# A delta-rule attention woven into a feed-forward: spreading VectorE's work of a step's first burst over the stretch behind it

## The chip, the cores and the metric

The kernel runs on one core of one Trainium2 chip. The metric is the device time in microseconds (us) of one execution. TensorE is called PE in the profile (its weight loads PEld), VectorE DVE, ScalarE ACT, GpSimd POOL and SyncE SP. `L867` is line 867 of the kernel before the change.

## The reference

Two blocks follow one another. The first is a delta rule over 768 positions, for 4 batches x 8 heads of width 48; the second is a feed-forward over the 3072 tokens of width 384 that the first one gives, with 2048 hidden units and a slope of its own for each unit below zero.

```python
k_n = k / (np.linalg.norm(k, axis=-1, keepdims=True) + 1e-06)
for t in range(S):
    y[:, :, t] = einsum('bhd,bhde->bhe', q[:, :, t], state)
    v_old = einsum('bhde,bhd->bhe', state, kt)
    state = state + bt * einsum('bhd,bhe->bhde', kt, vt - v_old)
x = attn_out.transpose(0, 2, 1, 3).reshape(B * S, H * D)
h = x @ w_in
g = np.maximum(h, 0.0) + alpha * np.minimum(h, 0.0)
return g @ w_out
```

All of it is in float32.

## The kernel before

**Steps.** The 768 positions are cut into 12 chunks of 64. A step is one chunk of one pair of batches, so there are 24 steps; even steps are the first pair of batches, odd steps the second. Within a chunk the recurrence is turned into matrix products and an inverse of a triangular matrix. A step n needs: keys times state (`through_state`, L793), whose result gives the right-hand side r (three subtractions, L812) and the masked matrix a_t (L521); `solve` (L824), whose result DVE weighs into u (L831); `outputs` (L836), copied to y (ACT at L848 up to step 15, DVE at L847 from step 16 on); and `next_state` (L853), subtracted from the state by DVE (L867, two instructions, one in the first steps). The state of a pair of batches is next read two steps later.

**Way of a step's result.** From step 8 on y is turned in 32x32 blocks by one DVE instruction (`turn_y`, L883, into z), and 16 small ACT copies (`rows_y`, L896) put the rows of z into xt, the feed-forward's input of a chunk. The odd step completes a chunk. z shares a tag of two buffers with r.

**The feed-forward** is a generator, `tail`, cut into parts; each part issues some matmuls of PE, and now and then DVE and ACT instructions. For chunks 2 to 7 (`ffn_in`, L989, and `ffn_out_fast`, L1051) a pair of hidden tiles takes 6 parts, one PSUM bank, one ACT relu (L1008) and two DVE instructions (L1010). From chunk 8 on (`ffn_in_fast`, L1201, `ffn_out_faster`, L1306) products are combined as in Strassen's scheme, and a pair i takes 6 parts: the common products (L1247) go into one PSUM bank that all pairs share, ACT copies the bank to a tile z_i (L1266; two tiles, called k_t and block in the profile, take turns), POOL adds three times in it (L1271), DVE adds it to the pair's own products (`total`, L1276), ACT takes the part below zero (L1281) and DVE puts in the slopes (L1285, two instructions). `Due` counts parts and says behind which part a total, a below and a slope is issued: the total of pair i stands some 3 parts behind the pair.

**Order of the work.** The order on every engine is written out by hand; the queues run in order. From step JOINED = 6 on, the loop at L1926 does for each step:

- `burst_a(n)`: PE gets outputs(n-1), next_state(n-1) and through_state(n) in a row, and then DVE gets all that reads them, in a row: the list `soon`, run by `now(soon)`.
- the first stretch: 8 to 12 parts of the feed-forward, woven with the lists that `stretch` (L1901) gets. `weave` (L1376) takes the items of each list in even spacing from a given share of the stretch on: `later`, what burst_a gave back (the loads of keys for step n+1, `load_late`, and of values for step n+3, `load_v`), from 0.5 on, rows_y from 0.4 or 0.5 on, pieces of the elimination (L593, L599, L566) from 0.3 on.
- `turn_round(n)`, and a second stretch of 10 to 18 parts.
- `burst_b(n)`: the solve of step n, and products for later steps, and a third stretch.

An odd step's first stretch holds 6 of the row copies of the even step before it, its second 2, its third 8; an even step's first stretch holds all 16 of the odd step before it. In steps 6 and 7 the feed-forward has two PSUM banks, from step 8 (NARROW) on four.

Of the kernel before, what the change touches and what calls it, by code (L numbers as in the profile page):

```python
# [32 lines left out]
C = 64  # L33
HB = 32
W_IN_P = 512
BUSY = 8
EARLY = 8
# [7 lines left out]
def kernel(  # L45
# [137 lines left out]
    def load_v(n):  # L183
        if n < N:
            v_raw[n] = work.tile([128, H, D], FP32, name="v_raw", bufs=3)
            fetch(v, n, v_raw[n])

    def load_late(n, halves=range(2)):

        if n < N:  # L190
            c, bp = steps[n]
            for t in halves:
                src = k[2 * bp + t, :, c * C : (c + 1) * C, :]
                src = src.rearrange("(g a) p d -> a p g d", a=2)
                for a in range(2):
                    dst = k_late[n % NKL].rearrange("p (g a) d -> a p g d", a=2)
                    nc.sync.dma_start(out=dst[a][half(t ^ a), :, 0:D], in_=src[a])
# [196 lines left out]
    def squares(n):  # L394
        if n < N:
            squared(n)
            norms(n)
# [363 lines left out]
    def between_1(n, p=None):  # L761
        return between((n, False, p))
# [30 lines left out]
    def through_state(n, p=None, p_y=None):  # L793
        if n >= N:
            return []
        c, bp = steps[n]
        if c == 0:
            rhs_[n] = by_parity(nv[n])
            return []
        p = region(p, G * (D + C), g=G)  # L800
        for g, a, t in quarters():
            nc.tensor.matmul(  # L802
                p[half(t ^ a), a, g], k_t[n][dims(a), g, half(t)], beside[bp][dims(a), t, g]
            )
        asked = query(n, p_y) if n < NARROW else []

        r = work.tile([128, 2, G, D], FP32, name="r")
        v_in = by_parity(nv[n])
        rhs_[n] = r

        def less(to, own, a):
            nc.vector.tensor_tensor(  # L812
                out=r[to, a], in0=v_in[to, a], in1=p[own, a, :, 0:D], op=ALU.subtract
            )

        return [
            lambda: less(slice(0, 128), slice(0, 128), 0),
            lambda: less(half(0), half(1), 1),
            lambda: less(half(1), half(0), 1),
            *asked,  # L820
            lambda: masked(n, p[:, :, :, D : D + C]),
        ]
# [13 lines left out]
    def outputs(n, p=None):  # L836
        c, bp = steps[n]
        p = region(p, G * D, g=G)
        for g, a, t in quarters():
            nc.tensor.matmul(  # L840
                p[half(t), a, g], a_t[n][half(t ^ a), a * G + g], us[n][half(t ^ a), a, g],
                start=(n < NARROW), stop=(n < NARROW or g == G - 1),
            )
        if c == 0 or n >= NARROW:
            ys[n] = work.tile([128, H, D], FP32, name="y")
            if n >= LATE:
                return [lambda: nc.vector.tensor_copy(out=by_parity(ys[n]), in_=p)]  # L847
            return [lambda: nc.scalar.copy(by_parity(ys[n]), p)]  # L848
        return [lambda: nc.vector.tensor_tensor(
            out=by_parity(ys[n]), in0=by_parity(ys[n]), in1=p, op=ALU.add  # L850
        )]

    def next_state(n, p=None):  # L853
        c, bp = steps[n]
        pieces, wide = [], n < 2 * NJ
        if c < NCH - 1:
            p = region(p, G * D, g=G)
            for g, a, t in quarters():
                nc.tensor.matmul(
                    p[half(a) if wide else dims(a), t, g], k_late[n % NKL][half(t ^ a), 2 * g + a, 0 : C if wide else D],  # L860
                    us[n][half(t ^ a), a, g],
                )


            def less(rows):
                x = state[bp][rows]
                nc.vector.tensor_tensor(out=x, in0=x, in1=p[rows], op=ALU.subtract)  # L867

            if wide:
                pieces = [lambda: less(slice(0, 2 * C))]  # L870
            else:
                pieces = [lambda: less(dims(0)), lambda: less(dims(1))]
        return pieces
# [3 lines left out]
    def turn_y(n):  # L877

        z = work.tile([128, 2, G, D], FP32, name="z", tag="r")
        z = z.rearrange("p a g d -> p (a g d)").rearrange("p (k r i) -> p r k i", r=4, i=HB)  # L880
        blocks_y[n] = z
        y = ys[n].rearrange("p h d -> p (h d)")
        nc.vector.transpose(  # L883
            z.rearrange("p r k i -> p k r i"), y.rearrange("p (k r i) -> p k r i", r=4, i=HB)
        )
# [485 lines left out]
    def part(gen, n):  # L1371
        for _ in range(n):
            next(gen, None)
            yield
# [49 lines left out]
    def is_turned(n):  # L1424
        return NARROW <= n < N - 1

    def burst_a(n):

        soon, later = [], []
        if n > NARROW:  # L1430
            b = asked_in.pop()
            y, z = b[:, :, G * C : G * C + WY], b[:, :, 0:WY]
        else:
            b = ps_big()
            y, z = b[:, :, 0:WY], b[:, :, WY : 2 * WY]
        if n > JOINED:
            soon += outputs(n - 1, y)
            soon += next_state(n - 1, z)
            if is_turned(n - 1) and n % 2 == 0:
                soon.append(lambda: turn_y(n - 1))  # L1440
            later.append(lambda: load_late(n + 1))
        if n < N:
            p = ps_big()
            y = ps_big()[:, :, 0:WY] if n < NARROW else None
            soon += through_state(n, p[:, :, 0 : G * (D + C)], y)
            if n < JOINED + 2:
                soon += between_1(n + 1, b[:, :, 2 * WY : 2 * WY + G * HB])
            if n == JOINED:
                soon += grams(n + EARLY, big[-1][:, :, WY : WY + G * C])
                later.append(lambda: squares(n + EARLY + 1))  # L1450
            later.append(lambda: load_v(n + 3))
        if is_turned(n - 1) and n % 2:
            soon.append(lambda: turn_y(n - 1))
        now(soon)
        return later

    def burst_b(n):

# [467 lines left out]
    for n in range(JOINED, N):  # L1926
        if n == NARROW:
            banks(2, 2)
        fill, share = FILL.get(n, FILLS[n % 2]), PIECES_OF.get(n, TURNS[n % NJ])
        extra = [[], [], []]  # L1930
        if n == JOINED:
            place(n + 1, (0,))
            extra[1] = [(weight_sums(1, 0, 3), 3)]
            extra[2] = [(weight_sums(0, 3, 4), 1)]
        elif n == JOINED + 1:
            extra[0] = [(weight_sums(1, 3, 4), 1, 0.6), (placing(n + 1, (1, 2, 3)), PLACING)]

        later = burst_a(n)
        if is_turned(n - 1):
            if n % 2:  # L1940
                rows = rows_y(n - 1)
                extra[0].append((part(rows, 6), 6, 0.5))
                extra[1].append((part(rows, 2), 2))
                extra[2].append((part(rows, 8), 8, 0.3))
            else:
                extra[0].append((rows_y(n - 1), 16, 0.4))
        stretch(fill[0], blocks, share[0], later, *extra[0], *put_off)
        put_off = []
        later = turn_round(n)
        if n == JOINED:  # L1950
            extra[1].append((placing(n + 1, (1, 2, 3)), PLACING))
        stretch(fill[1], blocks, share[1], later, *extra[1], soon=0.2)
        m, ends = (n + 6) // NJ, n % NJ == 2
        if ends and n > JOINED:
            for _ in blocks:
                assert False
            place(n + 2, (0,))
        later = burst_b(n) + [lambda: scale_v(n + 1)]
        if NARROW <= n < N - 2:
            later.append(lambda: turn_q(n + 2))  # L1960
        if n == JOINED:
            stretch(fill[2], blocks, share[2], later, *extra[2])
            for _ in blocks:
                assert False
            place(n + 2, (0,))
            place(n + 3, (0,))
            blocks = eliminate(m)
        else:
            if ends:
                blocks = eliminate(m) if m < N // NJ else iter(())  # L1970
            after = [(placing(n + 2, (1, 2, 3)), PLACING)]
            if n % NJ != 1:
                after.append((placing(n + 3, (0,)), 1))
            if n >= LATE:
                put_off, after = after, []
            stretch(
                fill[2], blocks, share[2], later, *after, *extra[2], soon=0.1 if n >= LATE else 0.5
            )
# [34 lines left out]
```

## Time and profile before

| | |
|---|---|
| median of 3 runs | 645.1 us (643.82 to 645.57) |
| the profiled execution | 646.49 us |
| its span | 644.8 us |
| PE busy | 628.0 us, 97% |
| DVE busy | 501.6 us, 78% |
| ACT busy | 309.2 us, 48% |
| POOL busy | 92.5 us, 14% |

The span runs from the first to the last instruction of the profiled execution; the rest of its 646.49 us lies around it. The granted clock is 1.0 over the span. Each step can be found in the trace by its outputs (L840), which burst_a begins with. The first bursts of the odd steps begin at 194.0 (step 7), 239.3, 286.4, 334.1, 381.8, 428.6, 475.0 (step 19), 521.4 (21) and 567.7 us (23); those of the even steps at 218.5 (step 8), 263.5, 309.9, 358.4, 405.6, 452.3, 498.7 and 545.1 us (22). `ffn_in_fast` (L1237, L1242, L1247) runs beside the odd steps from 19 on.

In the profile a matmul's end is modelled and matmuls overlap, so PE shows as busy through short waits; a wait shows in the distance from one start to the next. Two PE records stand for one float32 matmul.

### The profile page before, as it was taken

Reading aid. Unit: us, or ns where it says so; the run is one execution under the profiler, and the core shown is the slowest. Engines: PE = TensorE matmul, PEld = TensorE weight load, DVE = VectorE, ACT = ScalarE, POOL = GpSimd, SP = SyncE. Lnnn points to the kernel's source line nnn. Section 1 sums busy time; section 2 is a strip of 40 time slices with the busy share of each in tenths; the row PEclk is TensorE's granted clock in tenths of the full one; section 3 lists DMA queues with packets and bytes.
Section 4 is the critical chain, followed back from the end, with each engine's and each line's share of the span. In section 5 each row is a group of like instructions: output and inputs, shape, how many; then the busy total and the mean of one; then the engine's idle time right before and its main releaser. Section 6 shows DMA issues by size and latency. Waiting matters only on the chain.

```text
span 644.8 us, 21692 instructions
## 1 busy us (share of the span) xinstructions
PE 628.0 (97%) x9154; PEld 552.2 (86%) x9154; DVE 501.6 (78%) x1213; ACT 309.2 (48%) x816; POOL 92.5 (14%) x204
## 2 busy tenths in 40 slices
PE   6998999999999999999999999999999999999997
PEld 4687888566788988988988988989999989999997
DVE  4975998977999879859879858968978569577383
ACT  5887664344453243743644635325447256353240
POOL 6001211000000100001000000000044043061360
PEclk9999999999999999999999999999999999999999
DMA  7966835311353142243133121211220310100000
GB/s 117 297 133 159 238 68 140 82 32 34 56 78 56 36 70 48 39 64 51 33 63 57 26 52 26 39 39 25 42 53 9 57 21 6 36 2 1 25 1 25
DMA packets 145969, 39.27 MB, mean 61 GB/s; under 512 B 139040, under 2 KB 142256, under 8 KB 145872
## 3 DMA queue, kind: packets, MB, share of 16 engines
q1 hardware_dynamic: 144000, 37.40, 28.5%
q8 instruction: 72, 1.18, 0.7%
q10 hardware_dynamic: 1872, 0.49, 0.4%
q14 instruction: 25, 0.20, 0.1%
HBM read 33.14 MB, written 4.72 MB: 59 GB/s over the span
## 4 chain that ended last, share of the span: by engine, by line
PE 81%; DVE 8%; DMA 3%; SPq 3%; ACT 2%; issue 2%; POOL 1%; DVEq 0%; ACTq 0%; POOLq 0%
PE p_ffn L998 11%; PE p_ffn L1062 9%; PE p_more L1331 8%; PE p_more L1062 8%; PE p_more L998 7%; PE p_ffn L1041 7%; PE p_more L1247 4%; PE p_ffn L1331 3%; PE p_ffn L1237 3%; PE p_ffn L1242 2%; PE p_pair L733 2%; PE p_pair L840 2%; PE p_pair L802 2%; PE p_pair L1505 2%; PE p_pair L678 2%
## 5 line engine op out<-in xcount | busy, mean ns | idle before, releaser
L998 PE MATMUL p_ffn<-xt,w_in 128*128 128x256 f32 x528 | 124.1, 384 | 2.3 <-DVE act L1010 1.8
L998 PEld LDWEIGHTS p_ffn<-xt,w_in 128*128 128x128 f32 x528 | 97.4, 190 | 17.4 <-ACT wgt L718 1.6
L896 ACT COPY xt<-z 32x96 f32<-32x96 f32 x240 | 64.4, 269 | 47.9 <-DVE z L883 44.8
L998 PE MATMUL p_more<-xt,w_in 128*128 128x256 f32 x240 | 55.7, 382 | 0.0
L599 DVE TENSOR_TENSOR block<-block,prod 128x30 f32<-128x30 f32 (+9 forms) x150 | 49.8, 332 | 5.1
L1271 POOL TENSOR_TENSOR k_t<-k_t 128x128 f32<-128x128 f32 (+1 forms) x48 | 28.5, 593 | 166.9 <-ACT k_t L1266 164.4
L745 ACT COPY inv<-p_pair 32x256 f32<-32x256 f32 x40 | 14.5, 362 | 78.6 <-DVE u L831 45.1
L998 PEld LDWEIGHTS p_more<-xt,w_in 128*128 128x128 f32 x240 | 44.9, 190 | 6.3
L593 DVE TENSOR_TENSOR prod<-block 128x30 f32<-128x30 f32 (+9 forms) x150 | 48.5, 323 | 1.2
L418 POOL TENSOR_TENSOR beta_t<-beta_t,rec 128x8 f32<-128x8 f32 x24 | 6.1, 255 | 272.7 <-DVE rec L412 263.5
L1010 DVE SCALAR_TENSOR_TENSOR act<-act,al_t,p_ffn 128x256 f32<-128x256 f32 x72 | 31.1, 472 | 15.4 <-ACT act L1008 15.4
L1008 ACT ACTIVATE act<-p_ffn 128x512 f32<-128x512 f32 x36 | 21.4, 594 | 25.0 <-PE p_ffn L998 24.7
L1271 POOL TENSOR_TENSOR block<-block 128x128 f32<-128x128 f32 (+1 forms) x48 | 27.6, 576 | 14.1 <-ACT block L1266 11.5
L1237 PE MATMUL p_ffn<-xt,w_in 128*128 128x256 f32 x96 | 29.3, 387 | 0.0
L1062 PE MATMUL p_ffn<-w_out,act 128*128 128x192 f32 x160 | 28.2, 328 | 0.1
L1062 PEld LDWEIGHTS p_ffn<-w_out,act 128*128 128x128 f32 x160 | 26.2, 190 | 0.8 <-DVE act L1010 0.4
L1010 DVE SCALAR_TENSOR_TENSOR act<-act,al_t,p_more 128x256 f32<-128x256 f32 x40 | 17.2, 471 | 11.3 <-ACT act L1008 11.2
L831 DVE TENSOR_TENSOR u<-p_pair,wgt 128x384 f32<-128x384 f32 x24 | 13.2, 553 | 16.4 <-PE p_pair L827 10.2
L812 DVE TENSOR_TENSOR r<-v_raw,p_pair 64x192 f32<-64x192 f32 (+1 forms) x66 | 23.3, 352 | 2.4 <-PE p_pair L802 1.4
L554 ACT COPY same<-right 32x256 f32<-32x256 f32 x29 | 11.7, 403 | 22.7 <-DVE right L507 19.1
L1062 PE MATMUL p_more<-w_out,act 128*128 128x192 f32 x128 | 22.3, 326 | 0.0
L392 DVE TENSOR_REDUCE norm<-ksq 128x8 f32<-128x384 f32 x24 | 12.9, 545 | 12.0 <-ACT ksq L388 11.9
(256 smaller groups left out, 1480.7 us busy)
## 6 DMA issues: line engine op xcount, KB each, us to landing
w_out<-in_moe_w_in_dram SPq DMA_DIRECT2D x10, 512.0 KB, 5.4
v_raw<-in_v_dram SPq DMA_DIRECT2D x48, 96.0 KB, 2.7
kl<-in_k_dram SPq DMA_DIRECT2D x96, 48.0 KB, 2.6
out_dram<-o_sb SPq DMA_DIRECT2D x90, 48.0 KB, 1.6
space_out<-in_moe_w_out_dram SPq DMA_DIRECT2D x11, 384.0 KB, 4.7
ke_last<-in_k_dram SPq DMA_DIRECT2D x25, 96.0 KB, 2.6
qp<-in_q_dram SPq DMA_DIRECT2D x64, 32.0 KB, 2.3
w_out<-in_moe_w_out_dram SPq DMA_DIRECT2D x5, 384.0 KB, 4.2
```

The costliest lines, as they stand in the source:

```text
L593: nc.vector.tensor_tensor(out=prod, in0=r[:, 0:j, j : j + 1].to_broadcast([128, j, n]), in1=r[:, j : j + 1, j + 1 : HB].to_broadcast([128, ...
L599: nc.vector.tensor_tensor(out=r[:, 0:j, j + 1 : HB], in0=r[:, 0:j, j + 1 : HB], in1=prod, op=ALU.add)
L812: nc.vector.tensor_tensor(out=r[to, a], in0=v_in[to, a], in1=p[own, a, :, 0:D], op=ALU.subtract)
L896: nc.scalar.copy(to[quad(r), u, bp, t], z[quad(2 * t + u), r])
L998: nc.tensor.matmul(p_h[:, i], w_in[:, t, (f + i) * 128 : (f + i + 1) * 128], xt[:, t], start=(t == 0), stop=(t == KT - 1),)
L1010: nc.vector.scalar_tensor_tensor(out=g[:, i], in0=g[:, i], scalar=al_t[:, f + i : f + i + 1], in1=p_h[:, i], op0=ALU.mult, op1=ALU.add,)
L1041: nc.tensor.matmul(p_o[u], gs[f // 2][:, f % 2, u * 128 : (u + 1) * 128], w_out[:, f], start=(f == 0), stop=(f == FT - 1),)
L1062: nc.tensor.matmul(p, x(i), w(i), start=(i == 0), stop=(i == FP - 1))
L1237: nc.tensor.matmul(p[:, f * 256 : f * 256 + 256], w(2, f), xt[:, 2], start=True, stop=False)
L1247: nc.tensor.matmul(q[:, j], a, b, start=True, stop=True)
L1271: nc.gpsimd.tensor_tensor(out=dst, in0=a, in1=b, op=ALU.add)
L1331: nc.tensor.matmul(p, x(i), w(i), start=(i == 0), stop=(i == FP - 1))
```

## The change

Burst_a(n) no longer hands DVE everything at once. Its lists are now `soon` (outputs), `state_` (next_state), `later` (through_state and, in step 7, what follows it), `turn` (turn_y) and `loads`:

- In an odd step only the outputs' copy stays in the burst. The two state subtractions, the three subtractions for r, the mask and turn_y go, in this order, into the list that is woven into the first stretch.
- In an even step the outputs, the state subtractions and turn_y stay in the burst, and the subtractions for r and the mask go into the stretch.
- Step 6 keeps its order.
- The list begins at 0.0 of the stretch instead of 0.5, with `load_late` as its first item and `load_v` as its last.
- In an odd step the 6 row copies of the first stretch move to the second, which then holds 8; the third holds 8 as before.

```diff
-        soon, later = [], []
+        soon, state_, later, loads = [], [], [], []
...
+        turn = [lambda: turn_y(n - 1)] if is_turned(n - 1) else []
         if n > JOINED:
-            soon += outputs(n - 1, y)
-            soon += next_state(n - 1, z)
-            if is_turned(n - 1) and n % 2 == 0:
-                soon.append(lambda: turn_y(n - 1))
-            later.append(lambda: load_late(n + 1))
+            soon = outputs(n - 1, y)
+            state_ = next_state(n - 1, z)
+            loads.append(lambda: load_late(n + 1))
         if n < N:
...
-            soon += through_state(n, p[:, :, 0 : G * (D + C)], y)
+            later = through_state(n, p[:, :, 0 : G * (D + C)], y)
             if n < JOINED + 2:
-                soon += between_1(n + 1, b[:, :, 2 * WY : 2 * WY + G * HB])
+                later += between_1(n + 1, b[:, :, 2 * WY : 2 * WY + G * HB])
...
-            later.append(lambda: load_v(n + 3))
-        if is_turned(n - 1) and n % 2:
-            soon.append(lambda: turn_y(n - 1))
+            loads.append(lambda: load_v(n + 3))
+        if n == JOINED:
+            soon, later = soon + state_ + later, []
+        elif n % 2:
+            later = state_ + later + turn
+        else:
+            soon += state_ + turn
         now(soon)
-        return later
+        return loads[:1] + later + loads[1:]
...
                 rows = rows_y(n - 1)
-                extra[0].append((part(rows, 6), 6, 0.5))
-                extra[1].append((part(rows, 2), 2))
+                extra[1].append((part(rows, 8), 8))
                 extra[2].append((part(rows, 8), 8, 0.3))
...
-        stretch(fill[0], blocks, share[0], later, *extra[0], *put_off)
+        stretch(
+            fill[0], blocks, share[0], later, *extra[0], *put_off, soon=0.5 if n == JOINED else 0.0
+        )
```

More of the change, by code (lines that the diff above doesn't have):

```diff
@@ L1444, in burst_a @@
             y = ps_big()[:, :, 0:WY] if n < NARROW else None
-            soon += through_state(n, p[:, :, 0 : G * (D + C)], y)
+            later = through_state(n, p[:, :, 0 : G * (D + C)], y)
             if n < JOINED + 2:
-                soon += between_1(n + 1, b[:, :, 2 * WY : 2 * WY + G * HB])
+                later += between_1(n + 1, b[:, :, 2 * WY : 2 * WY + G * HB])
             if n == JOINED:
-                soon += grams(n + EARLY, big[-1][:, :, WY : WY + G * C])
-                later.append(lambda: squares(n + EARLY + 1))
-            later.append(lambda: load_v(n + 3))
-        if is_turned(n - 1) and n % 2:
-            soon.append(lambda: turn_y(n - 1))
+                later += grams(n + EARLY, big[-1][:, :, WY : WY + G * C])
+                loads.append(lambda: squares(n + EARLY + 1))
+            loads.append(lambda: load_v(n + 3))
[5 more added lines that the diff above has]
+            soon += state_ + turn
         now(soon)
-        return later
+        return loads[:1] + later + loads[1:]
     def burst_b(n):
```

## The prediction, made before the changed kernel was run

> **What bounds the kernel now.** I began with the page's busy shares, then took PE's waits from step 6 on, then the instructions in order of time around each wait.
>
> ```profile
> PE 628.0 (97%) x9154; PEld 552.2 (86%) x9154; DVE 501.6 (78%) x1213; ACT 309.2 (48%) x816; POOL 92.5 (14%) x204
> ```
>
> PE is the bound. The change touches no matmul, so it can win or lose only PE's waits. The view of waits, PE alone, from 173 us to the end, has these:
>
> ```profile
> PE p_ffn L998 <- DVE act L1010: 1.8, 2, 1.4
> PE p_more L1247 <- ACT block L1266: 0.9, 2, 0.4
> PE p_pair L733 <- issue: 0.6, 1, 0.6
> PE p_pair L802 <- ACT beside L457: 0.2, 1, 0.2
> ```
>
> The third (step 10, 328 us) waits for no engine: no edit here reaches it. The second stands in steps 19 and 21. In order of time, PE, DVE and ACT of step 19 (burst at 474.99):
>
> ```profile
> 480.59 0.38 PE L1242 MATMUL p_ffn<-k_t,w_in 128*128 128x128 f32 x2
> 481.42 0.49 PE L1247 MATMUL p_more<-xt,w_in 128*128 128x128 f32 x2 [0.44 <-ACT block L1266]
> 481.74 0.39 PE L1247 MATMUL p_more<-k_t,ke_pair 128*128 128x128 f32 x2
> ...
> 483.72 0.38 PE L1242 MATMUL p_ffn<-k_t,w_in 128*128 128x128 f32 x2
> 484.11 0.49 PE L1247 MATMUL p_more<-xt,w_in 128*128 128x128 f32 x2
> 484.43 0.39 PE L1247 MATMUL p_more<-k_t,ke_pair 128*128 128x128 f32 x2
> ```
>
> ```profile
> 476.22 0.56 DVE L847 COPY y<-p_pair 128x384 f32<-128x384 f32 x1 [0.64 <-ACT k_t L1281]
> 476.70 1.11 DVE L867 TENSOR_TENSOR beside<-beside,p_pair 48x384 f32<-48x384 f32 x2
> 477.82 1.09 DVE L812 TENSOR_TENSOR r<-v_raw,p_pair 128x192 f32<-128x192 f32 x3
> 478.94 0.69 DVE L521 TENSOR_TENSOR a_t<-p_pair,minus 128x512 f32<-128x512 f32 x1
> 479.54 0.57 DVE L883 STREAM_TRANSPOSE z<-y 128x384 f32<-128x384 f32 x1
> 480.04 0.65 DVE L1276 TENSOR_TENSOR act<-p_ffn,block 128x512 f32<-128x512 f32 x1
> 480.61 0.86 DVE L1285 SCALAR_TENSOR_TENSOR act<-k_t,al_t,act 128x256 f32<-128x256 f32 x2
> 481.39 0.68 DVE L1276 TENSOR_TENSOR act<-p_more,k_t 128x512 f32<-128x512 f32 x1
> 481.99 1.59 DVE L1285 SCALAR_TENSOR_TENSOR act<-block,al_t,act 128x256 f32<-128x256 f32 x2
> 483.50 0.68 DVE L1276 TENSOR_TENSOR act<-p_ffn,block 128x512 f32<-128x512 f32 x1
> ```
>
> ```profile
> 480.78 0.59 ACT L1266 COPY block<-p_more 128x512 f32<-128x512 f32 x1 [3.46 <-DVE act L1276]
> ```
>
> Read from the last fence backwards. ACT's copy into `block` waits 3.46 us for the total of the pair two before (L1276 at 480.04), which still reads that tile; that total stands behind the burst's operations (476.70 to 480.11). PE needs the copy, since the common products of all pairs share one bank. The price shows in the starts. PE's record after the two of L1242 comes 0.83 us behind (480.59 to 481.42) and 0.39 at the next pair (483.72 to 484.11); in step 23, which has no state subtractions, it comes at 572.95 to 573.17, 0.22. Each wait also spreads the record behind it (0.32 instead of 0.22). So step 19 loses 0.61 + 0.10 + 0.17 + 0.10 = 0.98. Step 21 has 0.81 and 0.38 at the same places: 0.59 + 0.10 + 0.16 + 0.10 = 0.95.
>
> The first wait's 1.40 is step 7's, at 203.26, with two banks:
>
> ```profile
> 199.04 0.50 DVE L849 TENSOR_TENSOR y<-y,p_pair 128x384 f32<-128x384 f32 x1
> 199.47 0.54 DVE L867 TENSOR_TENSOR beside<-beside,p_pair 128x384 f32<-128x384 f32 x1
> 199.94 1.07 DVE L812 TENSOR_TENSOR r<-v_raw,p_pair 128x192 f32<-128x192 f32 x3
> 201.04 0.69 DVE L521 TENSOR_TENSOR a_t<-p_pair,minus 128x512 f32<-128x512 f32 x1
> 201.64 0.68 DVE L952 TENSOR_TENSOR sums<-sums,act 128x512 f32<-128x512 f32 x1
> 202.24 0.87 DVE L1010 SCALAR_TENSOR_TENSOR act<-act,al_t,p_ffn 128x256 f32<-128x256 f32 x2
> ```
>
> **The change part by part.** No operation is added or taken away.
>
> *The spread list, odd steps.* Moved are two L867 (0.55 each), three L812 (0.35), L521 (0.69) and L883 (0.57): 3.4 us of DVE. In step 19 the stretch has 12 parts and the list 9 items, so between the parts DVE now gets: the y copy, total of pair 1, L867, slopes of pair 0, L867, two L812, total of pair 2, L812, slopes of pair 1, L521, L883, and then total of pair 3 in the second stretch. The total of pair 1 comes right after y, near 476.8 instead of 480.04, and ends near 477.5; PE fills the bank for the copy at 479.5; so the wait goes, and with it the second one, whose copy (483.49) was late behind row copies that PE's delay had put beside it: -0.98, and -0.95 in step 21. Step 23 has no such wait: 0.
>
> What is late next is the copy after that. It needs the total of pair 3, which has the same operations in front as before, all of them between 476.2 and 483.5, so it ends at 484.18 as before; and it needs ACT, which then has three row copies (0.27 each) behind z, which now ends just ahead of that total, near 483.5: 484.3. PE, 0.98 earlier, offers its bank at 484.37 (485.35 in the trace). The copy ends near 484.95, and PE wants it at 485.66 (486.64 - 0.98): 0.7 us to spare, which is the cover of this step.
>
> *The same in step 7.* ACT's relu (L1008) is freed of two copies that waited 3.15 us for L867, and the slopes behind it come ahead of five moved operations, near 201.1 instead of 202.24. So the wait at 203.26 shrinks from 1.40 to about 0.1. But DVE runs without a gap from 199 to 212.8, and the next things PE needs, the slopes at 204.50 and at 207.69, have the same operations in front as before. PE, earlier, waits there: the products of L1062 begin to need the 207.69 pair at 208.2, where PE stands now without time to spare. I take 0; the bounds are -1.4 (all of the wait gone) and +0.4 (half a pair of slopes, if the relu finds ACT busy with the two copies, 0.74, now put in the middle of the stretch).
>
> *Odd steps 9 to 17.* PE has no wait behind these bursts, only the start gaps that every burst has. Four banks, each 2.6 us of matmuls, cover a late slope by some 5 us; that is the cover, and with two banks step 7 shows what it costs without. 0; bounds -0.3 (the 0.33 that PE loses at 261 in step 9, where DVE again has no gap from 239 to 257, so I expect it to stay) to +0.5.
>
> *Even steps.* L812 x3 and L521, 1.75 us, go into the stretch; z and the row copies keep their place. No PE wait stands behind an even burst but step 8's gap at 235, which is not near it. 0, bounds -0.3 to +0.3.
>
> *Consumers of what comes later.* r is read by the solve and the banks are rewritten by burst_b, both two stretches on (10 to 15 us); a_t and the state are read in later bursts. All lie behind the 5 to 8 us of the first stretch.
>
> *Row copies.* Six per odd step (1.6 us of ACT) go one stretch later. The chunk is complete only with the even step's rows, which don't move: 0.
>
> *Loads on SP.* load_late (four DMAs) starts at the head of the stretch; its tile was read by matmuls already issued. load_v (two DMAs) goes from 3/4 to about 8/9 and waits for the third L812, as before, but that is itself some 2 us later. Behind it on SP stand load_q, and stores of o_sb. Keys and values land 2.6 and 2.7 us after issue and are used over 20 us later; o_sb has two buffers and about 20 us between uses. 0.
>
> Sum: -0.98 - 0.95 = -1.93. Against the profiled execution: 646.49 - 1.93 = 644.56. That one stands 1.39 above the median, of which 0.8 is the wait for issue; against the median 645.1 - 1.93, so **643.2**.
>
> **The rivals.**
>
> *A: half comes back.* The wait of step 19 goes, and the next copy or total takes its place. For it: DVE is busy 13.71 of the 15.00 us from 475 on, and PE running ahead finds it no earlier. Against: 0.7 us to spare. Price: 0.95 of 1.93 back, 644.1.
>
> [...] The row: two slopes take 0.86 us alone and 1.59 beside POOL's adds (L1271), 0.73 more, where waiting out all three adds (1.86) would make 2.72. [...]
>
> *B: step 7's wait goes too.* If the slopes at 207.69 don't hold PE, 1.4 more is won: 641.8. For it: that wait is the largest of the loop. Against: DVE has no gap there.
>
> *C, the other side: ACT is held behind z.* In odd steps turn_y is now eighth of nine items, and the first row copy stands at the head of ACT's second stretch; all behind it in ACT's queue waits for z: relus, and in steps 19, 21 and 23 the copies of the shared bank. For it: ACT already waits 44.8 us for z in 12 places. Against: z has only DVE's order before it and should end near 483.5. It decides from 0.7 us of lateness on: with z 2.0 late, 1.3 us in each of the three steps, 3.9 lost against 1.93 won: 647.1. Below 1.3 us late the kernel is still no slower.
>
> **How the numbers follow.** The forecast 0.44, A 0.16, B 0.20, C 0.20 (it stands also for a wait like it behind the other moved bursts). 0.3% is 1.94 us, so the line is at 643.16; that is about what a measurement of this kernel can tell from no change. The forecast lies on it: 0.23 of its 0.44 below, 0.21 above. Faster 0.43 (0.23 + B), same 0.37 (0.21 + A), slower 0.20. Range 641.5 to 646.5: from B with 0.3 for step 9, to C less its worst part. The forecast's own range is 642.3 to 644.0.
>
> **What would show it.** In steps 19 and 21 L1276 stands right behind L847, ACT's copy into block no longer waits for it, and PE has no 0.83 gap; PE waits for L1266 are gone from the list. In step 7 the L998 wait is shorter, and a wait near 205 or 208 takes its place. Wrong would be: PE waits for L1266 in step 23 or later in 19 and 21; ACT waits for L883 that are followed by late L1266 or L1008; a new PE wait in steps 9 to 18; load_v landing after its L773.

## The result, and the profile after

The changed kernel takes 642.6 us (median of 21 runs, 640.63 to 644.9) beside 645.1 us for the one before (21 runs). The ratio is 0.9961, with a 95% interval of 0.995 to 0.9973: 2.5 us faster, between 1.7 and 3.2. The profiled execution took 643.5 us, its span is 641.8 us.

The busy times are those of before within 0.8 us. In the page's line, PE's share of a shorter span is all that moves:

```profile
PE 627.9 (98%) x9154; PEld 552.0 (86%) x9154; DVE 500.8 (78%) x1213; ACT 309.9 (48%) x816; POOL 92.4 (14%) x204
```

The view of waits, PE alone, from 173 us to the end (us in total, times, longest), after the change:

```profile
PE p_pair L908 <- ACT mid L745: 0.5, 1, 0.5
PE p_ffn L998 <- DVE act L1010: 0.4, 1, 0.4
PE p_ffn L998 <- issue: 0.4, 1, 0.4
PE p_ffn L1062 <- DVE act L1010: 0.4, 2, 0.2
PE p_pair L802 <- ACT beside L457: 0.2, 1, 0.2
```

The two waits for L1266 are gone; so is the wait of L733 for issue; the 1.4 of step 7 has come apart into 0.5 (L908), 0.4 (L1062) and a little more. Setting the same matmul of both traces side by side shows where PE's position moves by more than 0.1 us:

| between | PE earlier (-) or later (+), us |
|---|---|
| start and step 7's burst | -0.32 |
| step 7 | -0.06 |
| step 8 | +0.19 (a wait for issue, larger than before) |
| step 12, in burst_b | -0.85 |
| step 19, second stretch | -0.98 |
| step 21, second stretch | -0.95 |
| all | -2.99 (rounding apart) |

The first row has no edit in it: the order up to step 7 is the same, and over the kernels below this part differed from before by -2.7 to +0.9 us. So the edited steps account for about 2.65 of the 2.99. The step 8 gap, too, was there at -0.3 to +0.3 in kernels that did not change step 8.

Step 19 in order of time, DVE, then ACT, then PE:

```profile
475.16 0.56 DVE L847 COPY y<-p_pair 128x384 f32<-128x384 f32 x1 [0.64 <-ACT k_t L1281]
475.63 0.68 DVE L1276 TENSOR_TENSOR act<-p_ffn,block 128x512 f32<-128x512 f32 x1
476.23 0.54 DVE L867 TENSOR_TENSOR beside<-beside,p_pair 48x384 f32<-48x384 f32 x1
476.69 0.87 DVE L1285 SCALAR_TENSOR_TENSOR act<-k_t,al_t,act 128x256 f32<-128x256 f32 x2
477.57 0.56 DVE L867 TENSOR_TENSOR beside<-beside,p_pair 48x384 f32<-48x384 f32 x1
478.14 0.72 DVE L812 TENSOR_TENSOR r<-v_raw,p_pair 128x192 f32<-128x192 f32 x2
478.90 0.69 DVE L1276 TENSOR_TENSOR act<-p_more,k_t 128x512 f32<-128x512 f32 x1
479.62 0.35 DVE L812 TENSOR_TENSOR r<-v_raw,p_pair 64x192 f32<-64x192 f32 x1
480.00 1.35 DVE L1285 SCALAR_TENSOR_TENSOR act<-block,al_t,act 128x256 f32<-128x256 f32 x2
481.28 0.68 DVE L521 TENSOR_TENSOR a_t<-p_pair,minus 128x512 f32<-128x512 f32 x1
481.88 0.56 DVE L883 STREAM_TRANSPOSE z<-y 128x384 f32<-128x384 f32 x1
482.37 0.65 DVE L1276 TENSOR_TENSOR act<-p_ffn,block 128x512 f32<-128x512 f32 x1
```

```profile
478.41 0.59 ACT L1266 COPY block<-p_more 128x512 f32<-128x512 f32 x1 [2.16 <-PE p_more L1247]
```

```profile
479.52 0.38 PE L1242 MATMUL p_ffn<-k_t,w_in 128*128 128x128 f32 x2
479.75 0.39 PE L1247 MATMUL p_more<-xt,w_in 128*128 128x128 f32 x2
```

The total of pair 1 (L1276 at 475.63) now stands right behind y. ACT's copy into block waits for PE's matmuls and no longer for that total, and PE's gap there is 0.23 instead of 0.83.

### The profile page after: what moved, and what is told of

It reads as the page before. It is cut to its first block, busy times and chain, and to the rows that moved or that the text cites. A ratio compares the mean times of both kernels' runs of the same rounds, so it can differ in the third digit from the quotient of the medians.

```text
span 641.8 us, 21687 instructions
## 1 busy us (share of the span) xinstructions
PE 627.9 (98%) x9154; PEld 552.0 (86%) x9154; DVE 500.8 (78%) x1213; ACT 309.9 (48%) x816; POOL 92.4 (14%) x204
## 4 chain that ended last, share of the span: by engine, by line
PE 82%; DVE 10%; ACT 2%; DMA 2%; issue 1%; SPq 1%; POOL 1%; ACTq 0%; DVEq 0%; POOLq 0%
PE p_ffn L998 11%; PE p_ffn L1062 9%; PE p_more L1331 8%; PE p_more L1062 8%; PE p_more L998 7%; PE p_ffn L1041 7%; PE p_more L1247 4%; PE p_ffn L1237 3%; PE p_ffn L1331 3%; PE p_ffn L1242 2%; PE p_pair L733 2%; PE p_pair L802 2%; PE p_pair L1508 2%; PE p_pair L840 2%; PE p_pair L501 2%; DVE act L1010 2%
## 5 line engine op out<-in xcount | busy, mean ns | idle before, releaser
L745 ACT COPY inv<-p_pair 32x256 f32<-32x256 f32 x40 | 14.5, 363 | 73.4 <-DVE u L831 40.9
L1062 PE MATMUL p_ffn<-w_out,act 128*128 128x192 f32 x160 | 28.4, 329 | 0.5 <-DVE act L1010 0.4
L1062 PEld LDWEIGHTS p_ffn<-w_out,act 128*128 128x128 f32 x160 | 26.2, 190 | 1.7 <-DVE act L1010 0.8
L1062 PE MATMUL p_more<-w_out,act 128*128 128x192 f32 x128 | 22.3, 326 | 0.0
L1041 PE MATMUL p_ffn<-w_out,act 128*128 128x384 f32 x64 | 21.8, 491 | 0.4 <-DVE more L1010 0.4
```

Of the source, the lines that this page charges most:

```text
L1041: nc.tensor.matmul(p_o[u], gs[f // 2][:, f % 2, u * 128 : (u + 1) * 128], w_out[:, f], start=(f == 0), stop=(f == FT - 1),)
L1062: nc.tensor.matmul(p, x(i), w(i), start=(i == 0), stop=(i == FP - 1))
```

## The experiments

Theory: the gain is the two waits in steps 19 and 21, and what costs there is one total that stands behind VectorE's burst. Rivals: many bursts give a little each; or ScalarE's row copies were the cause; or VectorE is so full that every microsecond on it counts. Later a second theory was needed for step 12. Times are ratios to the kernel before on the same chip, with 95% intervals.

| run | ratio | interval |
|---|---|---|
| steps 19 and 21 alone | 0.997 | 0.9959 to 0.9982 |
| all but 19 and 21 | 0.9997 | 0.9984 to 1.001 |
| early total | 0.9964 | 0.995 to 0.9977 |
| three masks more | 1.0019 | 1.0008 to 1.003 |
| one mask more | 0.997 | 0.9958 to 0.9982 |
| rows alone | 0.9987 | 0.9976 to 0.9998 |
| sums later | 0.994 | 0.9928 to 0.9952 |
| copies first | 0.9962 | 0.995 to 0.9974 |
| rows of 11 | 0.9985 | 0.9971 to 0.9999 |
| keys later | 1.0008 | 0.999 to 1.0025 |
| turn of 12 | 0.9988 | 0.997 to 1.0005 |
| masks in 12 | 0.9992 | 0.9975 to 1.001 |

**Steps 19 and 21 alone, and all but these.**

```diff
+SPREAD = (19, 21)          # the other run: range(7, 24) without 19 and 21
-        if n == JOINED:
-            soon, later = soon + state_ + later, []
+        if n not in SPREAD:
+            before, after = (turn, []) if n % 2 == 0 else ([], turn)
+            soon, later = soon + state_ + before + later + after, []
```

The row copies and the start of the list follow SPREAD in the same way.

> Steps 19 and 21 alone take the new order; all other steps keep the order of before. Theory (the gain is the two waits for the shared bank's copy, 0.98 and 0.95 us): 1.9 us faster than before, like the whole change; in the trace no PE wait for L1266, and step 7's wait of 1.4 us at L998 as before. Rival (many bursts give a little each, step 7 among them): 0.5 us faster or less.

> All steps from 7 on take the new order, but 19 and 21 keep the old one. Theory: within 0.3 us of before; both PE waits for L1266 stay, and step 7's wait comes apart into smaller ones that add up to nearly the same. Rival (many bursts give a little each): 1.5 to 2.5 us faster.

Measured: the first gains 0.3%, 1.9 us, and its trace has -0.98 and -0.95 at the two places and step 7's 1.4 as it was. The second is not told apart from before; its two waits for L1266 stay, and step 7's wait comes apart into 0.6 (at L908) and 0.4 (at L1062), as expected. In its profile PE also gains 0.85 in step 12, as in the changed kernel, which the time's interval (1.0 us faster to 0.6 slower) neither shows nor excludes. So the two steps carry most of the gain, and one more place deserves a look.

**The total alone.**

```diff
-            due.put(PER * (i + 1) + {0: PER, FP - 1: 2}.get(i, 3), total)
+            due.put(PER * (i + 1) + {0: PER, 1: 2, FP - 1: 2}.get(i, 3), total)
```

> The kernel before with one edit: the total of pair 1 in the fast feed-forward (L1276) is due one part earlier, so that it stands ahead of the odd steps' first burst on VectorE instead of behind it. Nothing is spread. Theory (what costs is that one total, behind the burst): about 1.9 us faster than before, no PE wait for L1266. Rival (VectorE's whole cluster of 4 us costs, whatever stands in front): the wait comes back at the next pair's copy, 0 to 0.8 us faster.

Measured: 0.9964, and -0.98 and -0.95 at the same two places, with the whole cluster of the burst left where it was. In steps 19 and 21, then, one instruction's place in VectorE's queue is the cause; the spreading is one way to get it there.

**How much lateness is covered.** The mask is written again over itself, with the same values:

```diff
-        nc.vector.tensor_tensor(
-            out=a_t[n]...
+        for _ in range(4 if n in (19, 21, 23) else 1):      # 2 in the other run
+            nc.vector.tensor_tensor(
+                out=a_t[n]...
```

> The changed kernel; in steps 19, 21 and 23 the mask (L521, 0.69 us) is done four times instead of once, so that z and the third total come 2.07 us later. Theory (0.7 us to spare in each of these steps, then one for one): 1.3 us and 0.1 for the spread record in steps 19 and 21, 0.6 in step 23, so 3.4 us slower than the changed kernel, about 0.9 us slower than before. Rival 1 (lateness of z is hidden further by PE's bank and the second tile): within 0.5 us of the changed kernel. Rival 2 (VectorE is full there, every microsecond counts): 6.2 us slower than the changed kernel.

> The changed kernel with the mask done twice instead of once in steps 19, 21 and 23: z and the third total 0.69 us later. Theory (0.7 us to spare): no PE wait for L1266 of more than 0.1 us, the time of the changed kernel within 0.3 us, so 2.2 us faster than before. Rival (every microsecond on VectorE counts there): 2.1 us slower than the changed kernel, the time of before.

Measured: with three more, 0.0058 above the changed kernel's ratio, 3.7 us; in the profile 1.65, 1.62 and 0.51 in steps 19, 21 and 23. (Lines stand one further on in this kernel.) ACT's copy into block comes behind three row copies, which waited for z, and PE waits for it:

```profile
484.91 0.49 PE L1248 MATMUL p_more<-xt,w_in 128*128 128x128 f32 x2 [1.38 <-ACT block L1267]
```

With one more, PE loses 0.20 and 0.18 in steps 19 and 21, a little more than the 0.1 that was expected. The traces give the cover. Against the changed kernel z ends 0.72 us later with one mask more and 2.16 us later with three (each mask takes 0.72 us from start to start, not 0.69). With 0.1 for the spread record, 0.72 - 0.20 + 0.1 and 2.16 - 1.65 + 0.1 both give 0.6 us. So neither rival held: in steps 19 and 21 lateness of z is free up to 0.6 us and costs one for one above; my 0.7 was 0.1 too large. In step 23 z came 1.78 us later and cost 0.51, so more is covered there.

**The row copies alone.**

```diff
-                extra[0].append((part(rows, 6), 6, 0.5))
-                extra[1].append((part(rows, 2), 2))
+                extra[1].append((part(rows, 8), 8))
```

> The kernel before with one part of the change: the six row copies of the odd steps go from the first stretch to the second; VectorE's order stays. Theory (the copies are beside the path): both waits for L1266 stay, the second of them perhaps without its 0.17 us, since no row copy stands in front of that copy; within 0.5 us of before. Rival (the row copies on ScalarE were what held the copy of the shared bank): 1 to 2 us faster.

Measured: 0.9987, 0.8 us faster (0.1 to 1.5) where 0.5 at most was expected. The first wait in steps 19 and 21 stays, which the rival did not have, and the second goes, 0.27 in each step with its spread record, as expected. What was not expected is 0.85 in step 12, the wait for issue. The row copies touch nothing there.

**Step 7.** The weight sum goes behind the slopes; in the second kernel the two copies into mid also come ahead of the state subtraction.

```diff
-            extra[0] = [(weight_sums(1, 3, 4), 1, 0.6), (placing(n + 1, (1, 2, 3)), PLACING)]
+            extra[0] = [(placing(n + 1, (1, 2, 3)), PLACING)]
+            extra[1] = [(weight_sums(1, 3, 4), 1, 0.9)]
...
+                    state_ = between_[: n % 2] + state_      # copies first only
```

> The changed kernel; one weight sum of step 7 (L985, 0.95 us on VectorE) goes from the first to the end of the second stretch, so that it no longer stands ahead of the slopes that PE needs at 205 and 208 us. Theory (VectorE without a gap is what holds PE there): the waits of 0.41 and 0.33 us at L1062 go, the one at L908 of 0.7 us stays; 0.8 us faster than the changed kernel. Rival (something else holds PE in step 7): within 0.2 us of the changed kernel in the profile's step 7.

> As the run with the weight sum later, and in step 7 the two copies into mid (L745) come first in the spread list, ahead of the state subtraction that shares their bank. Theory: the wait of L908 for them goes too, but the slopes of the next pair then hold PE: 0.9 to 1.2 us faster than the changed kernel. Rival (L908's wait was hidden by nothing): 1.5 us faster.

Measured: with the sum later, PE is 0.82 us earlier at step 8's solve than in the changed kernel, both waits of L1062 are gone and L908's stays:

```profile
PE p_pair L908 <- ACT mid L745: 0.6, 1, 0.6
PE p_ffn L998 <- issue: 0.5, 1, 0.5
PE p_ffn L998 <- DVE act L1010: 0.4, 1, 0.4
```

So VectorE's filled queue held PE in step 7. This is the fastest kernel of the study: 0.994 of the one before. The second missed: L908's wait went, but PE was only 0.32 earlier at the same place. Putting the copies first made VectorE stand idle for 0.32 us for ScalarE, which shares the bank with it, and delayed the slopes by about as much as PE had won (its waits for them at L1062 come to 1.0 us):

```profile
198.32 0.55 DVE L867 TENSOR_TENSOR beside<-beside,p_pair 128x384 f32<-128x384 f32 x1 [0.32 <-ACT mid L745]
```

**Step 12.** Among the kernels so far, the wait for issue was in every profile whose odd steps keep the row copies in the first stretch, and in none of the others. In step 11 of the kernel before, ACT and then DVE:

```profile
295.07 0.27 ACT L896 COPY xt<-z 32x96 f32<-32x96 f32 x1 [5.03 <-DVE z L883]
...
295.85 1.40 ACT L896 COPY xt<-z 32x96 f32<-32x96 f32 x5
...
298.01 0.60 ACT L1008 ACTIVATE act<-p_more 128x512 f32<-128x512 f32 x1
```

```profile
298.64 0.87 DVE L1010 SCALAR_TENSOR_TENSOR act<-act,al_t,p_more 128x256 f32<-128x256 f32 x2 [1.19 <-ACT act L1008]
```

The row copies wait 5.03 us for z at the head of ACT's queue; the relus come late behind them, and DVE, which has work for all of its time here, stands idle for 1.19 us. It stays about that much later through step 12, and L478, which turns the keys for the next matmuls (L501) there, ends 1.83 us ahead of the solve instead of 3.1 or more. Two theories from there to PE's gap: the key loads that follow L478 get in the way of the fetch of PE's instructions, or that fetch hangs on L478 itself.

```diff
# rows of 11: before, with step 11 alone as in the change
+                if n == 11:
+                    extra[1].append((part(rows, 8), 8))
+                else: ...
# keys later: before, step 12's key loads at the end of the third stretch
-        if bp == 1:
+        if bp == 1 and n != 12 + EARLY + 1:
             load_keys(c + 1)
# turn of 12: before, step 12's L478 in the first stretch
+            if n == 12:
+                later.append(lambda: turn_k(n + EARLY + 1))
# masks in 12: the changed kernel
+        for _ in range(3 if n == 12 else 1):
```

> The kernel before; in step 11 alone the six row copies go from the first stretch to the second. Theory (the wait for issue in step 12 hangs on step 11: row copies that wait for z hold back a relu, VectorE stands idle 1.19 us for it, runs later through step 12, and the key loads behind L478 fall together with the fetch of PE's instructions): VectorE's gap of 1.19 us in step 11 goes, L478 of step 12 begins some 3.9 us ahead of the solve instead of 2.6, and PE's gap of 0.84 us in step 12 goes; 0.85 us faster than before. The waits for L1266 stay. Rival (the gap in step 12 is chance, or comes from another step's order): it stays, no change.

> The kernel before; the eight key loads of step 12 alone are issued at the end of the third stretch instead of right behind L478. VectorE's order and lateness stay. Theory (it is the key loads that hold up the instruction fetch): PE's gap of 0.84 us in step 12 goes although L478 stays 2.6 us ahead of the solve; 0.85 us faster than before. Rival (the fetch is late for another reason, or any loads at that place do it, since the query loads move up to there): a gap of 0.5 us or more stays.

> The kernel before; in step 12 alone the turning of the keys (L478, with the key loads behind it) is issued in the first stretch instead of the second, some 5 us earlier; VectorE's total work is the same. Theory (PE's queue stands at the first L501, which reads what L478 writes, and the fetch of the next instructions starts only 1.1 to 1.4 us after L478 ends): the fetch starts earlier against the solve of step 12, PE's gap of 0.84 us goes, 0.85 us faster than before. Rival (the fetch is late for a reason that has nothing to do with L478): the gap stays.

> The changed kernel; in step 12 alone the mask is done three times instead of once, so that VectorE, L478 with it, runs 1.38 us later there. Theory (the fetch of PE's instructions hangs on L478): PE's gap in step 12, which the changed kernel doesn't have, comes back with 0.6 to 1.2 us; the rest of the trace as in the changed kernel; 0.6 to 1.2 us slower than it. Rival (no link): no gap, the time of the changed kernel.

Measured, from the traces: the end of L478 and the start of the instruction fetch (a packet of 16,384 bytes in queue q8) against the start of step 12's solve, and PE's longest distance from one matmul's start to the next there (0.32 is that of a burst's usual start):

| kernel | L478 ends | fetch starts | PE's gap, us |
|---|---|---|---|
| before | -1.83 | -0.41 | 0.84 |
| early total | -1.84 | -0.76 | 1.19 |
| keys later | -1.82 | -0.58 | 0.86 |
| masks in 12 | -1.62 | -0.41 | 1.23 |
| turn of 12 | -3.11 | -1.71 | 0.32 |
| rows of 11 | -3.21 | -1.78 | 0.32 |
| the change | -3.08 | -1.83 | 0.32 |

The key loads are cleared: without them the gap stays. Other loads are cleared by the same trace: no other DMA packet starts in the 2.9 us before its fetch. L478 decides, both ways: earlier in the kernel before, the gap goes (it came 1.3 us earlier, not the 5 that I had expected, as VectorE was late there too); later in the changed kernel, the gap comes back as the only new wait of over 0.2 us (L734 is L733 one line further on), and PE is 1.24 us later behind it than in the changed kernel, where 0.6 to 1.2 was expected:

```profile
PE p_pair L734 <- issue: 1.0, 1, 1.0
```

The times of these four agree in sign where an effect was expected, but only that of rows of 11 is clear of 1; 0.85 us is little beside intervals of 2 us and more, so this rests on the traces. In all four kernels of the table that have it, the gap stands behind the same PE instruction: 10,177 records of PE and PEld lie ahead of it.

The fetch's start alone does not give the size of the gap: it lasts 1.35 us in early total and 1.13 in masks in 12, and 0.92 in the other two kernels that have the gap. In the five traces with the gap (those four and steps 19 and 21 alone) PE goes on 1.28 to 1.55 us behind the end of the fetch, and PE runs dry 0.96 us behind the start of the solve; in the nine without it the fetch had ended 1.6 us or more ahead of that place.

## Why the prediction was right or wrong

*The time*: 643.2 was forecast, 642.6 measured, a gain of 1.93 against 2.5 (1.7 to 3.2); it fell to the side of "faster", which had 0.43. The time alone could not have shown that a term was missing, since 1.93 lies inside the interval of the gain.

*Steps 19 and 21*: right to the hundredth: 0.98 and 0.95 forecast, 0.98 and 0.95 found. The mechanism is shown twice, by the two steps alone and by the total alone. The order forecast for VectorE is the one in the trace, and the third total ends at 483.02 where 483.1 (484.18, less the 1.06 by which PE was already earlier) was due.

*What is late next*: right in kind, z and the row copies behind it; the cover was 0.6 us, not 0.7.

*Step 7*: the 0 held (-0.06), and for the reason given. The first wait shrank, and waits at the L1062 products took its place; the two copies into mid (L745), in the middle of the stretch, also gave L908 a wait of 0.5 that the prediction did not name (its bound of +0.4 had them in the way of a relu), and PE had it in place of the slopes' wait, not on top of it.

*Odd steps 9 to 17*: the step that failed, in two sentences of the prediction. "The third (step 10, 328 us) waits for no engine: no edit here reaches it" was wrong in the number, it is step 12's burst_b, and in substance. "Row copies ... 0" was wrong for step 11: with fewer copies that wait for z ahead of them, ACT gives VectorE its relus sooner (of VectorE's 1.19 us without work 0.25 is left), and that reaches PE in step 12 through L478 and the instruction fetch, 0.85 us. This is the difference between 1.93 and about 2.65 in the profile (1.93 + 0.85 + 0.06 - 0.19). Nor, as far as the profiles show, was the wait for issue part of what set the profiled execution 1.39 above the median, as the prediction had it: it stands in all four profiles of kernels that keep step 11's order of before with L478 where it was.

*Rivals*: A did not come, B neither. C's mechanism is real, as the masks show, but z was not late enough; with z 2.16 us late steps 19 and 21 lost 1.65 and 1.62, near the 1.3 that C had for 2.0. Two slopes beside POOL's adds took 1.35 us in steps 19 and 21 after the change, where the prediction's rows have 1.59, and 0.86 alone.

## What to carry to other kernels

Where an engine that bounds the time waits, look for the single instruction that it waits for and what stands ahead of it in its engine's queue; here moving one total by some four microseconds was worth as much in steps 19 and 21 (0.98 and 0.95 us) as spreading the work of every step. Small copies that wait for a late producer belong behind, not ahead of, what another engine waits for, even on an engine that is half idle: here ACT was busy for 48% of the span, and row copies that waited 5.03 us for z cost PE 0.85 us in step 12. The wait for "issue" in step 12 was not chance: in four traces it stood behind the same 10,177 records, and it came and went with L478, which ended 1.62 to 1.84 us ahead of the solve in the kernels of the table with it and 3.08 to 3.21 in those without. Ask what ended late a microsecond or two ahead of such a wait.

## What the runs showed of the hardware that was not expected

In step 12 PE paid for another engine's late instruction without a visible wait for it. Even in the kernels where L478 is late, it ends 0.65 to 0.87 us before the first L501 starts, so PE shows no wait for it. Yet a fetch of 16,384 bytes of instructions (queue q8) starts 1.07 to 1.50 us after L478's end in all fourteen traces of the study and lasts 0.92 us or more, and in the five where it started less than 0.8 us before the solve PE ran dry for 0.84 to 1.23 us. That it brings PE's instructions is the author's estimate from the counts: before has 72 such packets for 18,406 records of PE and PEld, 256 for each, though single ones lie 84 to 439 records apart. By what way the end of L478 sets the start of the fetch is not shown; that stays open.
